# Attention and token mixer on one core: in the first four head pairs the values, with a column of ones, move past standing unnormalised probabilities

## The chip, the core and the metric

The kernel runs on one core of a Trainium2 chip. The metric is the device time of one execution, in microseconds (us). A core has TensorE (PE, its matmuls; PEld, its weight loads), VectorE (DVE), ScalarE (ACT), GpSimd (POOL) and SyncE (SP, which here issues nearly all transfers).

## The reference

Causal attention over 4 batches of 12 heads (448 positions, 64 wide), then a token mixing and a channel mixing over the joined heads:

```python
scores = scale * q @ k.T ; scores above the diagonal = -1e9
attn = exp(scores - max) ; attn = attn / (sum(attn) + 1e-9)
x = heads of (attn @ v) side by side            # [4, 448, 768]
h = relu(x.T @ w_tok1) @ w_tok2 ; u = x + h.T   # 448 -> 256 -> 448
h2 = relu(u @ w_ch1) @ w_ch2 ; out = u + h2     # 768 -> 1536 -> 768
```

All inputs and the output are fp32.

## The kernel before

A list scheduler in the kernel file (class `Plan`) decides the order while the program is built. Every piece of work is a job with a cost per engine that may run it, the jobs it needs, the buffers that it holds and a rank; `emit` walks through modelled time and gives each free engine the ready job of the lowest rank. The table `NUDGE` shifts single ranks, `ONLY` pins single jobs to an engine, and `BIAS`, `FIRST` and `EARLY` say how strongly the plan prefers one engine over another (`FIRST` for jobs whose rank is under `EARLY`). Nothing of the plan runs on the chip: what runs is one fixed order for each engine. Until 75 us of modelled time TensorE gets a filler matmul (line 753, 512 bf16 columns, its result unused) whenever it has no ready job and has done little in the last few microseconds.

The 48 heads are worked on in 24 pairs (`g`), six pairs to a batch. For a pair:

- `load_pair` loads k and q in 32-wide blocks (lines 786) and v (lines 795 and 799, one tile `vraw` of 128 x 4 x 2 x 64); `prep` turns k and q with DVE (line 819).
- `heads`: scores by TensorE (line 849) in 14 pieces, put into four PSUM banks, one to a "round" r; rows 64 wide, so seven pieces c of 64 to 448 columns per pair. DVE scales, masks and takes the minimum of the negated scores (`low`, line 869), ACT takes the exponential in place and adds up the row sums (`expo`, line 881). An exponential with a sum leaves a second instruction on ACT, the accumulator read. Then, twice a pair, `guard` adds 1e-9 to the sums (line 900, or 898 on ACT) and `recip` inverts them (line 903).
- `by_tensor` (pairs 0 to 10): `norm` multiplies each of the seven pieces by its inverse (helper `copy`, line 522 on ACT, 524 on POOL or DVE), `flip` turns four 128 x 128 blocks of a round with TensorE into a bank (line 938), `evac` copies the bank into `pt`. Pairs 11 to 23 go `by_dma` instead.
- `values`: v stands in TensorE as 128 x 64 weights, one head in each half of the columns, and the turned probabilities move past it (line 1039); the output is [2 x 64, 448], channels on the partitions, and `evac` copies it in three pieces into `u`.
- `xturn`: four TensorE transposes of `u` (line 1085), a copy to `xh` and a difference to `xl` (line 533), positions on the partitions. The token matmuls (lines 1133 and 1166, `tokens`) take `xh` and `xl` after every second pair and add to `u`.

When a batch is through its six pairs, `split_u` and `channels` follow (line 1216), whose weights are loaded, converted, and written to a scratch in DRAM on the first use; for the last two batches products of sums of blocks are used (lines 1544 and 1635), and `finish` and `store` write the output.

Of the kernel before, what the change touches and what calls it, by code (L numbers as in the profile page):

```python
# [9 lines left out]
F32 = mybir.dt.float32  # L10
# [11 lines left out]
    "clear": {0: 1.17, 2: -0.46},  # L22
    "load_pair.blocks": {-2: -36.88, 0: 0.42, 6: -1.83, 8: 0.8, 10: 3.87, 12: 1.06, 16: 2.76, 18: 0.85, 20: 8.68,
        22: -5.03, 24: 1.22, 26: -13.46, 28: 25.22, 30: -1.36, 32: 0.08, 34: 2.56, 36: 1.63, 38: 0.03, 40: 4.62,
        42: 2.27, 44: 0.42},
    "load_pair.load": {0.5: 0.54, 2.5: 1.48, 4.5: 1.15, 8.5: 2.41, 10.5: -0.33, 12.5: -7.52, 14.5: -0.58,
        16.5: -0.42, 18.5: 0.8, 22.5: 4.72, 24.5: 5.31, 28.5: -0.38, 30.5: 1.82, 32.5: -1.93, 34.5: 1.62,
        36.5: -0.05, 38.5: -0.47, 40.5: -0.64, 42.5: 13.63, 44.5: -0.01, 46.5: -5.64},
    "narrow.load": {3.5: -0.17, 14: -19.05, 15: 3.09, 16: -4.11, 17: -9.28, 18: -1.53, 19: -0.04, 20: -13.62,
        22: -44.59, 23: 1.48, 24: 0.92, 25: -16.05, 26: -9.5, 28: 1.34, 29: -8.76, 30: -1.29, 31: 0.94, 32: -31.49,  # L30
        33: 0.91, 34: -1.47, 35: 12.16},
    "narrow.size": {3.5: 0.1, 12: 0.33, 13: 13.22, 15: -4.37, 17: 5.83, 18: 4.82, 19: -8.41, 20: 0.23, 21: 3.09,
        24: 9.62, 25: -4.57, 26: 24.43, 27: -9, 28: -32.9, 30: 16.89, 31: -1.07, 33: -5.06, 34: -0.96, 35: -12.41},
# [1714 lines left out]
```

## Time and profile before

| | us |
|---|---|
| median of 3 runs | 557.0 (556.42 to 558.07) |
| the profiled execution, its own time | 558.41 |
| its span, first to last instruction | 556.6 |
| busy PE / DVE / ACT / POOL | 546.4 / 420.6 / 328.0 / 165.3 |

The profile gives one execution. A busy PE counts fillers as well, and its matmuls are pipelined, so their recorded lengths overlap; steps between starts say more. "Idle before" is the time that an engine stood still ahead of an instruction, with what ended it. Lines are those of the kernel before.

### The profile page before, as it was taken

To read this page: it belongs to the slowest core of one execution; us is meant where nothing else is said; L and a number is where in the kernel's file an instruction comes from. 1 tells how busy PE (TensorE), PEld (TensorE's weight loads), DVE (VectorE), ACT (ScalarE), POOL (GpSimd) and SP (SyncE) were. 2 spreads that over 40 slices of the span, in tenths; PEclk is the share of its full clock that TensorE was granted. 3 is DMA by queue.
4 is the path that set the end of the run, shared out by engine and by line. 5 is a ranking of instruction groups with operands and counts; after the bars stand their busy time and mean duration, and the time that the engine had idled before them with its cause. 6 is when DMAs were issued, how large, how long until landed. Compare 5 with 4: busy or idle time off the path is not lost.

```text
span 556.6 us, 10289 instructions
## 1 busy us (share of the span) xinstructions
PE 546.4 (98%) x3470; PEld 461.7 (83%) x3475; DVE 420.6 (76%) x1002; ACT 328.0 (59%) x780; POOL 165.3 (30%) x256
## 2 busy tenths in 40 slices
PE   8998999999999999999999999999999999999997
PEld 4676887788888888877898888989999999999996
DVE  4777768778888877677887868798888859583855
ACT  4998888897785668779878695342232413140400
POOL 3363886355144223324033363133000011020000
PEclk9999999999999999999999999999999999999999
DMA  6777585698999798898999983179411111111137
GB/s 111 166 159 139 107 202 137 144 201 178 222 214 195 171 189 173 189 173 213 190 194 237 202 189 134 44 156 188 105 57 58 57 58 57 58 57 58 57 66 133
DMA packets 234724, 78.41 MB, mean 141 GB/s; under 512 B 208944, under 2 KB 224176, under 8 KB 234672
## 3 DMA queue, kind: packets, MB, share of 16 engines
q1 hardware_dynamic: 223056, 76.15, 62.2%
q10 hardware_dynamic: 11616, 1.61, 1.7%
q8 instruction: 27, 0.44, 0.3%
q14 instruction: 25, 0.20, 0.1%
HBM read 49.15 MB, written 14.94 MB: 115 GB/s over the span
## 4 chain that ended last, share of the span: by engine, by line
PE 80%; DMA 7%; DVE 5%; ACT 3%; SPq 2%; issue 2%; POOL 1%; ACTq 0%; DVEq 0%; POOLq 0%
PE ps L1216 25%; PE ps L1635 14%; PE ps L1544 12%; PE ps L1039 7%; PE ps L849 5%; PE ps L1166 4%; PE ps L1133 4%; DMA wraw<-in_moe_w_ch_dram 4%; PE ps L938 3%; PE ps L1615 3%; PE ps L1085 2%; PE ps L753 2%; SPq L786 2%; DMA out_dram<-kq 1%; DVE prob L869 1%
## 5 line engine op out<-in xcount | busy, mean ns | idle before, releaser
L1283 DVE TENSOR_TENSOR u<-ps,u 128x448 f32<-128x448 f32 x118 | 72.8, 621 | 39.7 <-PE ps L1635 31.0
L881 ACT ACTIVATE prob<-prob,stat 128x448 f32<-128x448 f32 (+6 forms) x168 | 83.7, 503 | 12.7 <-DVE stat L869 12.3
L869 DVE CUSTOM_DVE_ANT_0 prob<-ps,mask 128x448 f32<-128x448 f32 (+6 forms) x168 | 63.0, 415 | 11.5 <-PE ps L849 9.6
L524 POOL TENSOR_SCALAR prob<-prob,stat 128x448 f32<-128x448 f32 (+6 forms) x109 | 60.9, 575 | 32.0 <-DVE stat L903 26.6
L1216 PE MATMUL ps<-uh,wh 128*128 128x448 f32 x144 | 54.4, 378 | 0.2 <-POOL wh L524 0.2
L1216 PE MATMUL ps<-gh,wh 128*128 128x448 f32 x144 | 53.7, 373 | 0.0
L1216 PE MATMUL ps<-uh,wl 128*128 128x448 f32 x144 | 52.7, 366 | 0.3 <-DVE wl L533 0.3
L1216 PE MATMUL ps<-gh,wl 128*128 128x448 f32 x144 | 52.8, 367 | 0.1
L1216 PE MATMUL ps<-gl,wh 128*128 128x448 f32 x144 | 52.8, 366 | 0.0
L1216 PE MATMUL ps<-ul,wh 128*128 128x448 f32 x144 | 52.6, 366 | 0.0
L849 PE MATMUL ps<-kq,kq 64*64 64x448 f32 (+6 forms) x672 | 46.4, 387 | 2.8 <-DVE kq L819 1.5
L1039 PE MATMUL ps<-pt,vraw 128*64 128x448 f32 (+3 forms) x384 | 47.4, 386 | 0.6 <-ACT pt L522 0.4
L522 ACT ACTIVATE wh<-wf 128x768 fp32r<-128x768 f32 x23 | 19.1, 841 | 46.3 <-PE ps L1635 29.1
L1039 PEld LDWEIGHTS ps<-pt,vraw 128*64 128x64 f32 x384 | 25.9, 136 | 23.5 <-issue 12.3
L849 PEld LDWEIGHTS ps<-kq,kq 64*64 64x64 f32 x672 | 27.8, 132 | 20.8 <-issue 10.5
L528 ACT COPY pt<-pt 128x512 uint16<-128x512 uint16 (+1 forms) x50 | 38.8, 851 | 2.4 <-DMA pt<-prob 2.4
L522 ACT ACTIVATE u<-wf 128x768 fp32r<-128x768 f32 (+1 forms) x17 | 12.6, 749 | 37.1 <-PE ps L1544 18.3
L900 POOL TENSOR_SCALAR stat<-stat 128x3 f32<-128x3 f32 (+1 forms) x38 | 10.5, 276 | 77.6 <-ACT prob L881 69.9
L524 POOL TENSOR_SCALAR wh<-wf 128x768 fp32r<-128x768 f32 x19 | 17.1, 900 | 55.3 <-DVE wf L592 24.3
L533 POOL TENSOR_TENSOR wl<-wf,wh 128x768 fp32r<-128x768 f32 x14 | 26.5, 1889 | 22.2 <-ACT wh L522 21.4
L881 ACT ACTIVATION_READ_ACCUMULATOR prob<-prob,stat 128x1 f32 x168 | 32.4, 193 | 0.0
L528 ACT COPY prob<-prob 128x1024 uint16<-128x1024 uint16 x31 | 31.7, 1042 | 0.4 <-POOL prob L524 0.3
(209 smaller groups left out, 1431.7 us busy)
## 6 DMA issues: line engine op xcount, KB each, us to landing
wraw<-in_moe_w_ch_dram SPq DMA_DIRECT2D x24, 768.0 KB, 5.6
wf<-scratch SPq DMA_DIRECT2D x30, 384.0 KB, 3.4
scratch<-wf SPq DMA_DIRECT2D x24, 384.0 KB, 5.7
vraw<-in_v_dram SPq DMA_DIRECT2D x48, 96.0 KB, 2.8
kq<-in_k_dram SPq DMA_DIRECT2D x60, 56.0 KB, 4.4
kq<-in_q_dram SPq DMA_DIRECT2D x56, 56.0 KB, 2.5
gh<-in_k_dram SPq DMA_DIRECT2D x36, 56.0 KB, 2.4
gl<-in_q_dram SPq DMA_DIRECT2D x36, 56.0 KB, 2.5
```

The lines of the kernel that those rows point to most:

```text
L522: nc.scalar.activation(dst, src, AF.Copy, scale=scale)
L524: eng[e].tensor_scalar(dst, src, scale, 0.0, op0=ALU.mult, op1=ALU.add)
L528: nc.scalar.copy(out, in_)
L533: eng[e].tensor_tensor(dst, a, b, op=ALU.subtract)
L849: nc.tensor.matmul(scores[r].tile[lanes, WHERE[c]:WHERE[c] + wide(c)], lhsT=qe.tile[LANES[j], c * QC:(c + 1) * QC], rhs=ke.tile[LANES[j], ...
L869: nc.vector.tensor_tensor_reduce(out=part(c, r), in0=ps.tile[:, WHERE[c]:WHERE[c] + wide(c)], in1=mask[:, S - wide(c):], scale=-SCALE, sca ...
L881: nc.scalar.activation(part(c, r), part(c, r), AF.Exp, bias=stat.tile[:, 0, AT[c]:AT[c] + 1], scale=-1.0, accum_out=stat.tile[:, 1, AT[c]: ...
L1039: nc.tensor.matmul(ps.tile[LANES[j], c * QC:(c + nq) * QC], lhsT=s.tile[:, kb, j], rhs=view[:, o:o + nq, j], start=(kb == 0), stop=(n == 3),)
L1216: nc.tensor.matmul(ps.tile[:, :S], lhsT=x.tile[:, at_:at_ + P], rhs=y, start=(n == 0 and i == 0), stop=(n + 1 == w[2] and i == 2),)
L1283: eng[e].tensor_tensor(u, ps.tile[:, :S], u, op=ALU.add)
L1544: nc.tensor.matmul(ps.tile[:, :S], lhsT=l()[:, t * P:(t + 1) * P], rhs=r, start=(t == 0 and n == 0), stop=(t == half - 1 and n == 2),)
L1635: nc.tensor.matmul(ps.tile[:, :S], lhsT=l.tile[:, t * P:(t + 1) * P], rhs=r.tile, start=(n == 0), stop=(n == 3 * len(fs) - 1),)
```

## The change

For the pairs below `ROWS = 4` the row sums leave the exponentials, and `guard`, `recip` and the seven `norm`s go from between exponential and flip. The flipped, unnormalised blocks are written into `pt` in another layout, in which each 128 x 128 block of keys by queries is contiguous for a head. In the new `by_rows`, in place of `values` and `xturn`, these blocks are the standing operand and v moves past them: 20 matmuls of 65 columns, since v has a 65th column of ones, whose products are the row sums. The output has queries on the partitions, 4 x 65 columns to a bank, two banks to a pair. `guard` and `recip` work on those sums, and `norm` multiplies while it copies out of PSUM (one DVE instruction or four on ACT a bank). The result `x` lies in SBUF as `xturn` used to make it, so `xh` and `xl` are taken from there; four transposes and one copy make `u`. The ring of `stat` has four buffers for two; a kind of PSUM share "r" is added; the plan's preferences and the tables `NUDGE` and `ONLY` are other ones through the whole kernel.

```diff
@@ the tables NUDGE and ONLY: most entries redrawn @@
 NUDGE = {
-    "clear": {0: 1.17, 2: -0.46},
...
+    "by_rows.norm": {0: 12.57, 2: 1.57, 4: -6, 6: 2.02},
...
 ONLY = {
-    "by_tensor.evac": {0: "act", 16: "act", 20: "act"},
+    "by_rows.guard": {0: "act", 2: "act", 4: "act"},
+    "by_rows.hi": {-1: "act", 5: "pool"},
+    "by_rows.lo": {-1: "pool", 1: "pool", 3: "dve", 5: "pool"},
+    "by_rows.evac": {1: "dve"},
+    "by_rows.norm": {4: "dve", 6: "act"},
+    "by_rows.none": {5: "pool"},
...
@@ -241,9 +263,9 @@
-    BIAS = {"act": 200.0, "dve": 600.0, "pool": 0.0}
-    FIRST = {"act": 400.0, "dve": 600.0, "pool": 450.0}
-    EARLY = 3.5
+    BIAS = {"act": 175.0, "dve": 550.0, "pool": 0.0}
+    FIRST = {"act": 250.0, "dve": 350.0, "pool": 600.0}
+    EARLY = 6.0
@@ -474,14 +496,15 @@
+    STATS = 4
-    BUFS.update(stat=2, u=B, xh=1, xl=1, h1h=1, h1l=1, uh=NB, ul=NB, gh=NB * NF, gl=NB * NF)
+    BUFS.update(stat=STATS, u=B, xh=1, xl=1, h1h=1, h1l=1, uh=NB, ul=NB, gh=NB * NF, gl=NB * NF)
-    SHARE = {"s": 4, "t": 2, "a": 1, "m": 3, "w": 5}
+    SHARE = {"s": 4, "t": 2, "a": 1, "r": 2, "m": 3, "w": 5}
@@ -732,6 +755,10 @@
+    ROWS = 4
+    FROM = ((0,), (15, 17), (3, 6, 9), (4, 7, 10, 13))
+    INTO = (slice(5, 17, 3), slice(1, 13, 3), slice(0, 12, 3), slice(15, 19))
+    VW = D + 1
@@ -767,7 +794,8 @@
-        keep["vraw", n] = const.tile([P, NCH, 2, D], F32, tag=f"vraw_{n}", name=f"vraw_{n}")
+        keep["vraw", n] = const.tile([P, NCH, 2, VW], F32, tag=f"vraw_{n}", name=f"vraw_{n}")
+        nc.gpsimd.memset(keep["vraw", n][:, :, :, D:], 1.0)
@@ -793,11 +821,11 @@
-                        out=s.tile[:, :full, j, :],
+                        out=s.tile[:, :full, j, :D],
-                    out=s.tile[:TAIL, full], in_=src[b, 2 * t:2 * t + 2, full * P:].rearrange("h p d -> p h d")
+                    out=s.tile[:TAIL, full, :, :D], in_=src[b, 2 * t:2 * t + 2, full * P:].rearrange("h p d -> p h d")
@@ heads: the exps, and no guard and reciprocal for g < ROWS @@
                 def expo(e, c=c, r=r):
                     nc.scalar.activation(
                         part(c, r), part(c, r), AF.Exp, bias=stat.tile[:, 0, AT[c]:AT[c] + 1], scale=-1.0,
-                        accum_out=stat.tile[:, 1, AT[c]:AT[c] + 1],
+                        **({} if g < ROWS else {"accum_out": stat.tile[:, 1, AT[c]:AT[c] + 1]}),
                     )
                 a = plan.job({"dve": 82.0 + 0.975 * wide(c)}, low, [m, start], [ps, probs[r], stat], rank)
                 if start is None:
                     start = a
-                exps.append(plan.job({"act": 277.0 + 0.857 * wide(c)}, expo, [a], [probs[r], stat], rank))
+                exps.append(plan.job(
+                    {"act": (85.0 if g < ROWS else 277.0) + 0.857 * wide(c)}, expo, [a], [probs[r], stat], rank
+                ))
+            if g < ROWS:
+                rcs[r], exps = exps, []
+                continue
             for rg in RG:
                 if r == rg[-1]:
                     ats = [AT[c] for x in rg for c in ROUND[x]]
@@ -907,6 +940,7 @@
+        stats[g] = stat
@@ -920,8 +954,8 @@
         done = []
         prev = None
         for r, cs in enumerate(ROUND):
-            norms = []
-            for c in cs:
+            norms = list(rcs[r]) if g < ROWS else []
+            for c in cs if g >= ROWS else ():
                 def norm(e, c=c, r=r):
                     copy(e, part(c, r), part(c, r), stat.tile[:, 2, AT[c]:AT[c] + 1])
@@ -943,6 +977,10 @@
+                if g < ROWS:
+                    to = heads_of(pt)[:, :, INTO[r]].rearrange("p j n q -> p n j q")
+                    copy(e, to, ps.tile.rearrange("p (n j q) -> p n j q", n=4, j=2))
+                    return
@@ -953,7 +991,15 @@
+        if g < ROWS:
+            done.append(plan.job(
+                {"pool": 250.0}, lambda e: nc.gpsimd.memset(heads_of(pt)[:, :, 13], 0.0), done[:1], [pt], rank
+            ))
+    def heads_of(pt):
+        return pt.tile.rearrange("p b n q -> p (b n q)").rearrange("p (j o q) -> p j o q", j=2, q=QC)
@@ -1061,6 +1108,116 @@
+    def by_rows(g):
+        b, t = divmod(g, NT)
+        hf, o = divmod(t, NTH)
+        rank = 2.0 * g + RV
+        s, js = raws[g, "v"]
+        pt, pdone = turned.pop(g)
+        stat = stats.pop(g)
+        if t == 0:
+            utile[b] = slot("u")
+        u = utile[b]
+        if o == 0:
+            xs[b, hf] = slot("xh"), slot("xl"), []
+        sh, sl, done = xs[b, hf]
+        n = NCH * P
+        prev = None
+        ready = []
+        def view(s):
+            if o == 0 and s.tile is None:
+                make(s, [P, NCH, PART], F32R)
+            return s.tile[:, :, o * P:(o + 1) * P].rearrange("p (i m) d -> p i m d", i=2)
+        def x():
+            return heads_of(pt)[:, :, 15:19].rearrange("p i (m j) d -> p i m (j d)", m=2)
+        for i in range(2):
+            ps = share("r")
+            def pv(e, i=i, ps=ps):
+                bank(ps)
+                cols = heads_of(pt).rearrange("p j o q -> p j (o q)")
+                for m in (2 * i, 2 * i + 1):
+                    for j in range(2):
+                        to = (2 * (m % 2) + j) * VW
+                        for kb, at in enumerate(FROM[m]):
+                            w = cols[:, j, at * QC:(at + 2) * QC]
+                            nc.tensor.matmul(
+                                ps.tile[:, to:to + VW], lhsT=w, rhs=s.tile[:, kb, j],
+                                start=(kb == 0), stop=(kb == m),
+                            )
+            def guard(e, i=i, ps=ps):
+                sums = ps.tile[:, :4 * VW].rearrange("p (a w) -> p a w", w=VW)[:, :, D]
+                at = stat.tile[:, 1, 4 * i:4 * i + 4]
+                if e == "act":
+                    nc.scalar.activation(at, sums, AF.Copy, bias=1.0e-9)
+                else:
+                    nc.vector.tensor_scalar(at, sums, 1.0e-9, None, op0=ALU.add)
+            def recip(e, i=i):
+                nc.vector.reciprocal(stat.tile[:, 2, 4 * i:4 * i + 4], stat.tile[:, 1, 4 * i:4 * i + 4])
+            def norm(e, i=i, ps=ps):
+                to = x()[:, i].rearrange("p m (j d) -> p (m j) d", j=2)
+                by = ps.tile[:, :4 * VW].rearrange("p (a w) -> p a w", w=VW)[:, :, :D]
+                f = stat.tile[:, 2, 4 * i:4 * i + 4]
+                if e == "dve":
+                    nc.vector.tensor_tensor(to, by, f.unsqueeze(2).broadcast_to([P, 4, D]), op=ALU.mult)
+                else:
+                    for n in range(4):
+                        copy(e, to[:, n], by[:, n], f[:, n:n + 1])
+            prev = plan.job({"pe": (6, 14)[i] * 125.0}, pv, js + pdone + [prev], [ps, s, pt, stat], rank)
+            a = plan.job({"act": 100.0, "dve": 95.0}, guard, [prev], [ps, stat], rank)
+            a = plan.job({"dve": 85.0}, recip, [a], [stat], rank)
+            ready.append(plan.job({"act": 4 * 118.0, "dve": dve1(4 * D)}, norm, [a], [ps, stat, pt], rank))
+        rank = 2.0 * g + RX
+        def hi(e):
+            copy(e, view(sh), x())
+        def lo(e):
+            minus(e, view(sl), x(), view(sh).bitcast(F32))
+        ps = share("t")
+        def turn(e):
+            bank(ps)
+            for m in range(NCH):
+                at = min(m * P, S - P)
+                nc.tensor.transpose(ps.tile[:, at:at + P], x()[:, m // 2, m % 2], ident)
+        def evac(e):
+            if t == 0:
+                make(u, [P, NT, S], F32)
+            copy(e, u.tile[:, t], ps.tile[:, :S])
+        first = [u_ready[b, 0]] if t else []
+        a = plan.job({"pe": pe(0, 0, 0, 0)}, turn, ready, [ps, pt], rank, turn=True)
+        u_ready[b, t] = plan.job({"act": act_ps(S), "dve": dve1(S)}, evac, [a] + first, [ps, u], rank)
+        c = plan.job(
+            {"act": act_sb(n), "dve": dve2(n), "pool": pool1(n)}, hi, ready + done[:1], [pt, sh], rank, lock=True
+        )
+        d = plan.job({"dve": dve1(n), "pool": pool2(n)}, lo, [c] + done[1:2], [pt, sh, sl], rank, lock=True)
+        done += [c, d]
+        if o == NTH - 1:
...
@@ -1702,8 +1859,11 @@
-        values(g)
-        xturn(g)
+        if g < ROWS:
+            by_rows(g)
+        else:
+            values(g)
+            xturn(g)
```

## Rows read from the trace of the kernel before

**Rows 1.** Busy time of each engine by stretch, granted clock, DMA

```profile
6.82:26.84 20.02, 18.71 (x174) 11.68 (x175) 14.81 (x64) 17.41 (x58) 6.02 (x14) 1.00 0.73 150
26.84:57.00 30.16, 27.91 (x266) 20.00 (x264) 23.66 (x94) 27.06 (x90) 15.83 (x35) 1.00 0.71 145
57.00:540.00 483.00, 481.65 (x2960) 417.09 (x2960) 371.17 (x824) 282.21 (x634) 139.73 (x187) 1.00 0.63 141
540.00:556.60 16.60, 12.71 (x65) 11.04 (x63) 9.65 (x19) 0.00 (x0) 0.00 (x0) 0.96 0.74 131
```

**Rows 2.** The same stretches, filler matmuls alone (line 753): PE, PEld

```profile
6.82:26.84 20.02, 5.60 (x22) 2.09 (x23) 1.00 0.73 150
26.84:57.00 30.16, 2.01 (x7) 0.88 (x9) 1.00 0.71 145
```

**Rows 3.** PE in order of time: start, length, line, [idle before <-releaser]

```profile
8.49 1.47 PE L753 MATMUL ps<-mask 128*128 128x512 bf16 x6
11.06 1.09 PE L849 MATMUL ps<-kq,kq 64*64 64x448 f32 x12 [1.09 <-DVE stat L903]
12.08 0.66 PE L938 MATMUL ps<-ident,prob 128*128 128x128 f32 x4
...
16.30 1.09 PE L849 MATMUL ps<-kq,kq 64*64 64x448 f32 x12 [0.16 <-DVE kq L819]
...
22.27 1.24 PE L753 MATMUL ps<-mask 128*128 128x512 bf16 x5
...
24.96 1.95 PE L1039 MATMUL ps<-pt,vraw 128*64 128x448 f32 x16
26.84 1.75 PE L849 MATMUL ps<-kq,kq 64*64 64x448 f32 x28
...
40.37 0.77 PE L1085 MATMUL ps<-ident,u 128*128 128x128 f32 x4 [0.75 <-DVE u L524]
...
51.62 1.09 PE L849 MATMUL ps<-kq,kq 64*64 64x448 f32 x12 [1.30 <-DVE kq L819]
```

**Rows 4.** ACT, DVE and POOL in order of time, first pair

```profile
8.61 0.67 ACT L881 ACTIVATE prob<-prob,stat 128x448 f32<-128x448 f32 x1 [4.54 <-DVE stat L869]
9.19 0.19 ACT L881 ACTIVATION_READ_ACCUMULATOR prob<-prob,stat 128x1 f32 x1
9.28 0.60 ACT L881 ACTIVATE prob<-prob,stat 128x384 f32<-128x384 f32 x1
...
10.45 0.24 POOL L900 TENSOR_SCALAR stat<-stat 128x3 f32<-128x3 f32 x1 [5.89 <-ACT prob L881]
...
11.16 1.00 POOL L524 TENSOR_SCALAR prob<-prob,stat 128x448 f32<-128x448 f32 x2 [0.47 <-DVE stat L903]
```

**Rows 5.** Groups by line, first 75 us: busy us, mean ns

```profile
L881 ACT ACTIVATION_READ_ACCUMULATOR prob<-prob,stat 128x1 f32 x56 | 10.9, 194 | 0.0
L524 POOL TENSOR_SCALAR prob<-prob,stat 128x448 f32<-128x448 f32 (+6 forms) x35 | 17.6, 519 | 8.2 <-DVE stat L903 8.2
L522 ACT ACTIVATE prob<-prob,stat 128x384 f32<-128x384 f32 (+5 forms) x13 | 6.2, 504 | 0.0
L903 DVE RECIPROCAL stat<-stat 128x3 f32<-128x3 f32 (+1 forms) x15 | 2.3, 163 | 0.3 <-POOL stat L900 0.2
L524 DVE TENSOR_SCALAR u<-ps 128x256 f32<-128x256 f32 (+2 forms) x9 | 2.2, 301 | 0.2 <-PE ps L1039 0.2
```

**Rows 6.** Single weight loads and narrow matmuls in order of time

```profile
18.99 0.28 PE L1039 MATMUL ps<-pt,vraw 128*64 128x64 f32 x4
19.04 0.23 PE L1039 MATMUL ps<-pt,vraw 128*64 128x64 f32 x2
19.20 0.20 PEld L938 LDWEIGHTS ps<-ident,prob 128*128 128x128 f32 x2
19.26 0.25 PEld L938 LDWEIGHTS ps<-ident,prob 128*128 128x128 f32 x2
```

**Rows 7.** DVE in order of time: the turn of the fourth pair's q

```profile
25.94 0.65 DVE L819 STREAM_TRANSPOSE kq<-gl 128x448 f32<-128x448 f32 x1 [0.59 <-DMA gl<-in_q_dram]
```

More of the change, by code (lines that the diff above doesn't have):

```diff
@@ L29 @@
[L29 to L33, printed above, removed]
@@ new lines @@
+    "by_rows.none": {1: -3.02, 5: 4.57},
+    "tokens.tok1": {4.5: 0.45, 8.5: -7.6, 12.5: 18.35, 16.5: -3.76, 20.5: -0.04, 24.5: 2.1, 28.5: 6.85, 32.5: 34.5,
+        36.5: 0.83, 40.5: -6.33, 44.5: -0.03, 48.5: -10.19},
+    "tokens.relu": {-5: 1.89},
+    "tokens.lo": {-5: -1.47},
+    "tokens.plus": {-5: -0.02},
+    "by_rows.twice": {5: 2.24},
+    "tokens.tok2": {8.5: -7.84, 12.5: -3.52, 16.5: -4.03, 20.5: 2.43, 24.5: 8.09, 28.5: -0.92, 32.5: 1.73,
+        40.5: 0.87, 44.5: 4.29, 48.5: 0.74},
@@ new lines @@
+    "channels.relu": {-6: 11.02},
+    "channels.down": {28.5: -29.26, 28.75: 0.16, 29: 0.23, 29.25: 2.64, 29.5: -4.01, 29.75: 4.65, 36: 0.22,
[5 rows of a table added]
+    "add.plus": {-6: 24.05},
+    "store.turn": {-5: 35.2},
+    "store.send": {-5: -4.69},
+    "reread.load": {-4.95: 1.16, -4.94: 0.34, -4.92: 6.14, -4.91: -0.19, -4.9: 3.76},
+    "group.up": {54: 17.53, 54.18: 5.85, 54.54: -1.47, 54.9: -7.06, 74.25: 12.25, 74.43: -3.66, 74.61: -9.5,
+        74.79: 0.12, 74.97: 0.12, 75.15: -0.81},
+    "hidden.relu": {-6: -0.57},
@@ L147 @@
+    "spared.hi": {-4.9: -12.62},
+    "spared.lo": {-4.9: -0.23},
+    "finish.plus": {-6: 1.64},
+    "finish.turn": {-6: -3.91},
+    "finish.evac": {-6: -1.13},
+    "finish.send": {-6: 2.16},
 }
@@ new lines @@
+    "heads.guard": {10: "pool", 14: "dve", 16: "pool", 20: "dve", 22: "dve", 24: "act", 30: "act", 32: "pool",
+        34: "pool", 42: "pool", 44: "pool", 46: "act"},
+    "xturn.<lambda>": {9: "dve", 19: "dve", 21: "dve", 27: "act", 31: "act", 33: "act", 39: "act", 43: "dve",
+        45: "act"},
+    "split_u.hi": {12.5: "act", 36.5: "act"},
+    "split_u.lo": {12.5: "pool", 36.5: "dve", 48.5: "dve"},
+    "by_tensor.norm": {14: "pool", 18: "pool", 20: "act"},
+    "xturn.twice": {13: "act", 17: "pool", 33: "act"},
@@ L1018 @@
     turned = {}
+    stats = {}
     def values(g):
@@ L1063, in values, with twice, none @@
         u_ready[b, t] = plan.job({"act": 110.0 + act_ps(S), "dve": 120.0 + dve1(S)}, evac, [prev] + first, [ps, u], rank)
+    def by_rows(g):
[80 more added lines that the diff above has]
+        if o == NTH - 1:
+            def twice(e):
+                x = sh.tile[:, NCH - 1]
+                copy(e, x[:TAIL], x[P - TAIL:].bitcast(F32))
+            def none(e):
+                x = sl.tile[:TAIL, NCH - 1]
+                copy(e, x, mask[:TAIL, :PART])
+            c = plan.job({"act": act_sb(PART), "pool": pool1(PART)}, twice, done[:], [sh], rank)
+            done += [c]
+            done += [plan.job({"act": act_sb(PART), "pool": pool1(PART)}, none, done[:], [sl], rank)]
```

213 lines of the change are left out of this document (100 added, 113 removed), and 47 rows, old and new, of the table NUDGE.

## The prediction, made before the change was run

> **What bounds the kernel now.** I read the busy times by stretch first [rows 1]. From 57 to 540 us TensorE stands still for 483.00 - 481.65 = 1.35 us at a granted clock of 1.00 (2.4 GHz), so there only less TensorE work would help, and the change takes none away. The tail, 540 to 556.6, stands still for 3.9 us behind the last additions and stores; the change does not touch it. What can be won lies before 57 us. There I took the fillers out [rows 2]: 22 in the first stretch, 7 in the second. Five in a row last 1.24 us [rows 3], of which the last one's own length overlaps; the step is about 0.215, so they cover 4.7 and 1.5 us. With the idle time (20.02 - 18.71 = 1.3 and 30.16 - 27.91 = 2.25) TensorE does nothing useful for 6.0 us between 6.8 and 26.84 and for 3.75 us between 26.84 and 57: 9.8 us in all. That is the most that an earlier supply of the first pairs can give.
>
> Then the order in time says what is late [rows 3]. After the first scores there are fillers from 8.49 and a stand until 11.06; the first flip comes at 12.08. The other engines tell why [rows 4]: the first exponential runs from 8.61 to 9.28, but its flip waits for three exponentials with their reads, for the guard at 10.45, an inverse, and the norm on POOL at 11.16. ACT is busy for 17.41 of the 20.02 us of that stretch [rows 1], so there the softmax sets the pace, not TensorE. In the second stretch two stands end otherwise: at 40.37 on a copy of values by DVE, at 51.62 on k and q just turned by DVE [rows 3], that is, on loads.
>
> **The change, part by part.**
>
> *TensorE, values.* Before, a pair takes from 24.96 to 26.84, 1.88 us [rows 3], as 16 records: an fp32 matmul leaves two, and the two heads share the array. After, there are 20 matmuls with 128 x 128 fp32 weights, thus 40 loads and 40 records of 65 columns, one behind the other. No row has 128 weight columns with so few moving ones, so I bound the step. From below by the moving columns: 64 of them step from 18.99 to 19.04 [rows 6], so 65 take about 0.055, 2.2 us a pair. From above by a transpose, which pairs the same 128 x 128 fp32 load with 128 columns: the loads at 19.26 and the next one, whose two take 0.25 us together where one takes 0.20 - 0.06 = 0.14, stand 0.11 us apart [rows 6], 4.4 us a pair. Between them: the first two loads of that flip start at 19.20 and 19.26 [rows 6], 0.06 apart, with nothing moving yet that the second would wait for. That is the nearest to a load alone, so I take 0.06: 2.4 us a pair, 0.52 more than before, **+2.1 us** for four pairs (bounds +1.3 and +10.1).
>
> The Trainium skill, "TensorE: Matmul & The Clock Gate", section "LDWEIGHTS (loading the stationary operand)", lets a load take its columns divided by 1.2 in nanoseconds, 107 for 128 columns; by it the term would be (40 x 0.107 - 1.88) x 4 = +9.6 us and the whole sum +3.4, 560.4, close to the upper bound. The trace has a second such load started 0.06 us after the first [rows 6], which speaks against it, though a load that starts early could still be slow to end.
>
> *TensorE, the rest.* Flips stay four a round and the four transposes stay; +0. Instead of turning probabilities for the values, nothing else is added.
>
> *ACT.* 28 accumulator reads go (7 x 4 pairs). A read lasts 0.194 [rows 5], but it starts 0.09 before its exponential ends and the next starts 0.10 before the read ends [rows 4], so each step shrinks by about 0.10: 2.7 us in all (at most 5.4).
>
> *Norms.* 28 of the seven-piece norms go. In the first 75 us POOL ran 35 for 17.6 us and ACT 13 for 6.2 us [rows 5]; at 0.5 each, 28 are 14 us of engine time, by their shares about 10 on POOL and 4 on ACT. In return DVE or ACT multiplies 256 PSUM columns twice a pair. The nearest row is DVE's copy of values, 0.30 for pieces of 64 to 256 columns [rows 5]; I take 0.4, so 8 x 0.4 = 3.2 us on DVE, which is busy for 14.81 of 20.02 [rows 1] and hides it; without that room, as much is late on `x`, and behind it the token matmuls. Bounds: 0.3 and 1.0 (four ACT pieces). Guard and inverse (0.16 [rows 5]) stay two each a pair, only later in the chain; the three copies of values into `u` become one.
>
> *No cost that I count:* a memset per pair on POOL and two for the ones at the start, since POOL is idle for 14 us of the first stretch [rows 1]; the 65-wide `vraw`, whose transfers keep their pieces of 256 bytes; `xh` and `xl` out of SBUF in place of PSUM. The stat ring of four can only take a wait away. No transfer is added.
>
> *What the path gains.* The first flip can follow its exponential, at about 9.5 instead of 12.08. For each of the four pairs the guard, the inverse and the norm (0.24 + 0.16 + 0.5, with waits of 0.5 us for the inverse [rows 4]) come out from between exponential and flip, and go behind the values. ACT, the pacing engine, loses 2.7 + 4 = 6.7 us of work in the opening. I reckon that the first stretch recovers 4.9 of its 6.0 us: all but some 1.1 us around the first exponential, where TensorE has nothing but q and k that are not there yet. TensorE's work for pairs 0 to 2, 3 x (1.75 scores + 4 x 0.45 flips + 2.4 values + 0.5 transposes) = 19.4 us, fits into the 20 us until pair 3's q is turned at 25.94 to 26.6 [rows 7]. In the second stretch the stands on loads remain; I take 1.3 of 3.75.
>
> **Sum.** 2.1 - 4.9 - 1.3 = -4.1 us. The profiled execution took 558.41 us (span 556.6 and 1.8 around it), 1.4 above the median of the runs shown; -4.1 makes 554.3 of it and 552.9 of the median 557.0. I predict 553.0. The redrawn order of all later work can move the 1.35 and 3.9 us of stands after 57 us by perhaps 1.5 either way.
>
> **The rivals.**
>
> *A. The weight loads bind: slower.* With a load every 0.11 us, as in the flips [rows 6], the values cost 4.4 us a pair. With the same recovery the sum is 10.1 - 6.2 = +3.9: 560.9. It decides from 0.086 us a load on, where 4 x (40 x 0.086 - 1.88) eats the 6.2 us. For it: in every transpose load and matmul step together at 0.11. Against it: the 0.06 of the first two loads, and that 128 moving fp32 columns explain the 0.11 alone, twice the 0.05 of 64 columns [rows 6]. It is the case that the Trainium skill's rule ("TensorE: Matmul & The Clock Gate") describes.
>
> *B. The loads pace the opening: the gain is given back.* What is done earlier before 26.84 becomes a longer wait for pairs 4 to 6, whose k and q come when they came before. If all 4.9 us of the first stretch return as waits before 57, the sum is 2.1 - 1.3 = +0.8: 557.8. For it: the stands at 16.30 and 51.62 end on DVE's turn of new q or k [rows 3], and pair 3's q ended 0.59 us of DVE's idling [rows 7]. Against it: behind the opening lie the token matmuls, which wait for no load of q or k, and from 57 us on TensorE has more work than it can do [rows 1], so work pulled forward has a backlog to start on.
>
> *C. The waits were not the softmax's.* If the copies out of PSUM and the token weights on ACT hold the flips, half is recovered: 2.1 - 3.1 = -1.0, 556.0. For it: ACT still has exponentials and copies in the same queue. Against it: 12.08 against 9.28 for the first flip, where no such copy stands before it.
>
> **How the numbers follow.** Chances: the forecast 0.62, A 0.12, B 0.14, C 0.12. The forecast's own range is 550.5 to 555.2 (recovery of 4.5 to 8, the order +-1.5). The range over the cases is 549.0 to 559.0: below, 8 us recovered at the lower price of the values with the order in its favour (557.0 - 8 + 1.3 - 1.5 = 548.8); above, B with the order against it; it leaves out most of A. Two measurements of this kernel can be told apart from about 0.3%, 1.7 us. The forecast is faster; B and C within 0.3%, but for a 0.02 of B that the order makes slower; A is slower: 0.62, 0.24, 0.14.
>
> **What the profile would show.** Right: far fewer than 29 fillers and 3.5 us of idling between 6.8 and 57 us; the first flip before 10 us; 40 value loads of a pair in about 2.4 us; the first channel matmul some 4 us earlier. Wrong: value records that step at 0.11 (A); the stands before 57 grown and ended by turns of k or q (B); the same fillers with flips released by ACT copies (C). A granted clock below 1.00 in the opening, where fewer fillers run, would break all of it: at half the clock each microsecond of such a stretch costs half of one.

## The result: slower, 561.05 us against 557.18

The changed kernel took 561.05 us (median of 7, 559.7 to 561.95), the kernel before 557.18 beside it: 1.0061 of before, 95% interval 1.0035 to 1.0087. By the medians that is 3.9 us slower (3.4 by the ratio, 1.9 to 4.8 by its interval), where 553.0 was predicted. The profiled execution took 559.93 us, 1.1 under its median; its span is 558.1.

Windows of the changed kernel, columns as in [rows 1], and under "..." those of its fillers alone (line 780; columns as in [rows 2]). In its line numbers 877 are scores, 909 exponentials, 972 flips, 1149 values, 1194 the four transposes and 847 DVE's turns of k and q; in other runs the lines shift by a few.

```profile
6.82:26.84 20.02, 19.02 (x199) 15.86 (x199) 14.09 (x56) 15.44 (x41) 4.69 (x7) 1.00 0.74 163
26.84:57.00 30.16, 30.16 (x286) 25.94 (x287) 21.22 (x83) 24.70 (x77) 15.36 (x29) 1.00 0.63 125
57.00:540.00 483.00, 483.00 (x3003) 416.96 (x2996) 384.94 (x869) 291.95 (x659) 110.36 (x138) 1.00 0.64 141
...
6.82:26.84 20.02, 1.19 (x4) 0.39 (x4) 1.00 0.74 163
26.84:57.00 30.16, 3.41 (x12) 1.17 (x12) 1.00 0.63 125
```

Idle time and fillers (0.215 us each) before 57 us fell from 9.75 us to 1.0 + 0 + 16 x 0.215 = 4.4. Taken alone this looks like the forecast come true: 5.3 us recovered, 6.2 predicted. (One of the 29 fillers counted before had started at 6.51, ahead of the first scores, so it is 0.2 less.) But TensorE is full of something else. Its order in time:

```profile
6.96 1.75 PE L877 MATMUL ps<-kq,kq 64*64 64x448 f32 x28 [0.69 <-DVE kq L847]
9.56 0.63 PE L972 MATMUL ps<-ident,prob 128*128 128x128 f32 x4 [0.86 <-ACT prob L909]
...
23.09 4.58 PE L1149 MATMUL ps<-vraw,pt 128*128 128x65 f32 x40
27.51 0.60 PE L972 MATMUL ps<-ident,prob 128*128 128x128 f32 x4
...
73.81 0.47 PE L1373 MATMUL ps<-uh,wh 128*128 128x448 f32 x1
```

The first flip comes at 9.56 in place of 12.08 [rows 3]; about 9.5 was forecast. The granted clock of both stretches is 1.00, as before. The values of a pair take from 23.09 to 27.51, 4.42 us, not 2.4: with 1.88 before [rows 3], +10.2 us for four pairs. The first channel matmul starts at 73.81; before it was 74.75 (the 74.75 line below). So 0.9 us of the 4 forecast are there. The weight loads of this kernel by line and form (busy us, mean ns | idle before), values first:

```profile
L1149 PEld LDWEIGHTS ps<-vraw,pt 128*128 128x128 f32 x160 | 18.3, 192 | 0.4 <-ACT pt L545 0.3
L972 PEld LDWEIGHTS ps<-across_ident,prob 128*128 128x128 f32 x88 | 10.1, 142 | 1.3 <-issue 0.6 <-ACT prob L909 0.2
```

A value load of 128 columns is recorded as 0.19 us long and the next starts about 0.11 us later (4.42 / 40); the flips' loads, from which the prediction took its price, are recorded as 0.14.

From the trace of before, two lines that the prediction did not use, the start of its channel matmuls (order in time) and ordinary fp32 loads of 128 columns (groups by form):

```profile
74.75 0.47 PE L1216 MATMUL ps<-uh,wh 128*128 128x448 f32 x1
```

```profile
L1133 PEld LDWEIGHTS ps<-xl,w1hi 128*128 128x128 f32 x96 | 18.3, 191 | 0.1
```

Apart from those of transposes, every 128 x 128 fp32 load of before is recorded as 187 to 191 ns long. So the trace of before already told these loads from the flips'; but neither recorded length is the step of 0.11.

### The profile page after: what moved, and what is told of

It is laid out like the page before. It is cut to its first block, busy times and chain, and to the rows that moved or that the text cites. A ratio compares the mean times of both kernels' runs of the same rounds, so it can differ in the third digit from the quotient of the medians.

```text
span 558.1 us, 10391 instructions
## 1 busy us (share of the span) xinstructions
PE 549.7 (98%) x3554; PEld 471.4 (84%) x3554; DVE 430.4 (77%) x1027; ACT 333.4 (60%) x775; POOL 134.5 (24%) x198
## 4 chain that ended last, share of the span: by engine, by line
PE 96%; DMA 1%; ACTq 1%; DVE 0%; issue 0%; ACT 0%; DVEq 0%
PE ps L1373 32%; PE ps L1792 15%; PE ps L1701 11%; PE ps L877 8%; PE ps L1086 7%; PE ps L1290 6%; PE ps L1323 5%; PE ps L972 4%; PE ps L1149 3%; PE ps L1772 3%; PE ps L1242 2%; ACTq L1846 1%; DMA kq<-in_q_dram 1%; PE ps L780 1%; DMA out_dram<-kq 1%; PE ps L1194 0%
## 5 line engine op out<-in xcount | busy, mean ns | idle before, releaser
L1373 PE MATMUL ps<-gh,wh 128*128 128x448 f32 x144 | 53.6, 372 | 0.0
L877 PE MATMUL ps<-kq,kq 64*64 64x256 f32 (+6 forms) x672 | 46.7, 388 | 0.7 <-DVE kq L847 0.7
L551 ACT COPY pt<-pt 128x512 uint16<-128x512 uint16 (+1 forms) x57 | 45.3, 865 | 3.4 <-DMA pt<-prob 3.4
L545 ACT ACTIVATE wh<-wf 128x768 fp32r<-128x768 f32 x20 | 16.5, 839 | 43.2 <-PE ps L1792 32.6
L1086 PE MATMUL ps<-pt,vraw 128*64 128x448 f32 (+3 forms) x320 | 39.5, 387 | 0.0
L547 POOL TENSOR_SCALAR prob<-prob,stat 128x448 f32<-128x448 f32 (+6 forms) x60 | 34.7, 593 | 18.1 <-DVE stat L936 18.0
L1086 PEld LDWEIGHTS ps<-pt,vraw 128*64 128x64 f32 x320 | 21.1, 136 | 19.5 <-issue 11.9
L556 POOL TENSOR_TENSOR wl<-wf,wh 128x768 fp32r<-128x768 f32 x15 | 28.6, 1907 | 35.4 <-ACT wh L545 34.5
L1792 PE MATMUL ps<-u,wh 128*128 128x448 f32 x108 | 30.9, 367 | 0.0
L1373 PEld LDWEIGHTS ps<-uh,wh 128*128 128x128 f32 x144 | 27.0, 188 | 3.4 <-issue 1.1
L1373 PEld LDWEIGHTS ps<-gh,wh 128*128 128x128 f32 x144 | 27.1, 188 | 2.8 <-DVE u L1331 0.2
```

The costliest lines, as they stand in the source:

```text
L547: eng[e].tensor_scalar(dst, src, scale, 0.0, op0=ALU.mult, op1=ALU.add)
L551: nc.scalar.copy(out, in_)
L556: eng[e].tensor_tensor(dst, a, b, op=ALU.subtract)
L877: nc.tensor.matmul(scores[r].tile[lanes, WHERE[c]:WHERE[c] + wide(c)], lhsT=qe.tile[LANES[j], c * QC:(c + 1) * QC], rhs=ke.tile[LANES[j], ...
L1086: nc.tensor.matmul(ps.tile[LANES[j], c * QC:(c + nq) * QC], lhsT=s.tile[:, kb, j, :D], rhs=view[:, o:o + nq, j], start=(kb == 0), stop=(n ...
L1373: nc.tensor.matmul(ps.tile[:, :S], lhsT=x.tile[:, at_:at_ + P], rhs=y, start=(n == 0 and i == 0), stop=(n + 1 == w[2] and i == 2),)
```

## The experiments

Ratios are to the kernel before, run on the same chip, with their 95% intervals. Some kernels keep the order of all instructions and change only what an instruction is; those are compared most directly. Where the planner had to draw another order, it is said.

**1. What a value load costs.** The changed kernel with its first four pairs' value matmuls in four forms, and then halves in all four pairs:

```diff
 (changed kernel, by_rows, pv)
-  matmul(ps.tile[:, to:to + VW], lhsT=w, rhs=s.tile[:, kb, j], ...)
+  for h in LANES:      # weights in two halves of 64 columns
+      matmul(ps.tile[h, to:to + VW], lhsT=w[:, h], rhs=s.tile[:, kb, j], ...)
```

> The changed kernel, its value matmuls of the first four pairs in four widths: pair 0 moves 33 columns (half the channels are left out), pair 1 moves 65 as before, pair 2 moves 128 (both heads, so its values are other numbers), pair 3 moves 65 columns past each 128 x 128 block given as two blocks of 64 weight columns in the two halves of the array. Theory (the loads of 128 fp32 weight columns set the step): 0.11 us a record in pairs 0, 1 and 2 alike, so 40 records in 4.4 to 4.5 us each, and 0.056 us for the two halves together in pair 3, as in the kernel before, 2.2 to 2.3 us for 80 records. Rival (the moving columns, or a fixed cost of each matmul, set the step): by columns 0.057 : 0.112 : 0.22 us in pairs 0, 1, 2 and no gain in pair 3; by a fixed cost per record 0.11 in pairs 0, 1, 2 and 0.22 for the two halves in pair 3.

One execution took 558.83. Its value matmuls in order of time: pair 0 moves 33 columns, pair 1 65, pair 2 128; pair 3 has halves.

```profile
16.85 3.21 PE L1150 MATMUL ps<-vraw,pt 128*128 128x33 f32 x28
23.07 4.58 PE L1166 MATMUL ps<-vraw,pt 128*128 128x65 f32 x40
39.42 3.39 PE L1155 MATMUL ps<-vraw,pt 128*128 128x128 f32 x28
48.99 2.55 PE L1161 MATMUL ps<-vraw,pt 128*64 128x65 f32 x80
```

28 records last 3.21 us with 33 columns and 3.39 with 128: the columns that move are nearly free. Twice as many records with half the weight columns take 2.55 us where 40 whole ones take 4.58, so it is no fixed cost of each record either. The load theory holds.

> The changed kernel in the same order, but in all four pairs each 128 x 128 block stands as two blocks of 64 weight columns, one in each half of the array. Theory (the weight loads of the values are what made the change slower): 2.2 us less TensorE work a pair, 9 us in all; all of it lies before 57 us, where the order has fillers left, and shows at the end nearly in full: 552 to 554 us, ratio to the kernel before 0.990 to 0.995. Rival (the redrawn order of the rest, or the tail, made it slower): the values are faster, but the end stays at 558 to 561, ratio 1.00 to 1.006.

558.62 (median of 12), 1.0040 (1.0024 to 1.0055). The theory (552 to 554) failed; the time lies where the rival had it. The values now cost 2.5 to 2.6 us a pair, close to the 2.4 that the prediction assumed and to the 20 x 0.125 us by which the plan drew this order, and the time is still 2.2 us over before, not 4 under. Some 7.5 us of TensorE time went, and the end came only 1.7 us earlier by the medians (1.2 by the ratios, whose intervals overlap). So the load price alone does not explain the miss: a second step failed. TensorE by stretch, and what it waited for:

```profile
6.82:26.84 20.02, 17.93 (x294) 1.00 0.75 155
26.84:57.00 30.16, 26.84 (x358) 1.00 0.69 134
```

```profile
27.02 0.66 PE L972 MATMUL ps<-across_ident,prob 128*128 128x128 f32 x4 [1.35 <-ACT prob L909]
...
44.47 1.09 PE L877 MATMUL ps<-kq,kq 64*64 64x448 f32 x12 [0.30 <-DVE kq L847]
...
54.97 1.09 PE L877 MATMUL ps<-kq,kq 64*64 64x448 f32 x12 [1.73 <-DVE kq L847]
```

2.1 and 3.3 us of idling, with the same 16 fillers (3.4 us): 8.2 to 8.9 of the 9.75 us of before are back (three of the 16 filler matmuls are not in the trace and may be counted as idling too). In the changed kernel they were missing because dear values filled them. In the two stretches ACT's exponentials end 2.2 us of stands, turns of k and q 2.0.

**2. Does TensorE work in the opening reach the end at all?** Before, with 12 more fillers a pair, 10.3 us, put in at the values of the first four pairs:

> The kernel before with 12 more filler matmuls (2.6 us at 0.215) ahead of the values of each of the first four pairs, 10.3 us in all: the TensorE time that the weight loads of the changed kernel add, in the old order. Theory (the opening has waits that take up most of added TensorE work): +3 to +6 us, ratio 1.005 to 1.011. Rival (TensorE is the bound there too, each us lands at the end): +9 to +10.3 us, ratio 1.016 to 1.019.

565.44, 1.0159 (1.0135 to 1.0182): 8.9 of the 10.3 us arrive, nearly the rival's 9 to 10.3, and the theory failed. TensorE time that is added at the values of the old order reaches the end; in the changed kernel's order, where 7.5 us taken away gave back 1.2 to 1.7, most of it came back as stands.

**3. What holds the opening: the softmax or the loads?** One part taken away at a time, the order kept:

```diff
 in heads and by_tensor, no normalisation for g < 4 (its jobs stay, but issue nothing)
-  accum_out=stat.tile[:, 1, AT[c]:AT[c] + 1],
+  **({} if g < 4 else {"accum_out": stat.tile[:, 1, AT[c]:AT[c] + 1]}),
...
+  if g < 4: return      # in guard, recip and norm
 in load_pair, light loads for pairs 1 to 6
+  if 0 < g < 7:
+      eng[e].dma_start(out=s.tile.rearrange("p c d -> p (c d)"),
+          in_=src[b, 2 * t:2 * t + 2].rearrange("j (a x) d -> (j a) (x d)", x=7))
+      return
   for n in range(4):    # four strided transfers
```

> The kernel before in its own order, with the row sums, the additions to them, the inverses and the seven multiplications of the first four pairs left out, so these pairs stay unnormalised. It shows what the softmax's waits are worth without any TensorE cost. Theory (the opening waits for these steps): the idle 1.3 us of the first stretch and part of the 2.25 us of the second go, but the fillers, which are fixed in the order, stay: -1 to -3 us, ratio 0.995 to 0.998. Rival (the opening is paced by loads and by copies out of PSUM): no change, ratio 0.999 to 1.001.

> The kernel before, its order the same, with k and q of pairs 1 to 6 read by one transfer in DRAM order (rows of 1792 bytes) in place of four in blocks of 128 bytes; these pairs work on other numbers. SyncE's issue time falls from 2.0 to about 0.5 us a load, and the transfer itself is shorter. Theory (the loads pace the opening; what TensorE gains or loses there is taken from or given to waits on them): the stands that end on DVE's turns of k and q go, 2 to 4 us, ratio 0.993 to 0.997. Rival (the order of ACT, DVE and POOL paces it): under 1 us, ratio 0.999 to 1.001.

> The changed kernel with the same light loads for pairs 1 to 6. There TensorE has only 4.4 us of fillers and idling left between 6.8 and 57 us. Theory (loads pace the opening, but here the slow values fill most of the wait): 0 to 2 us less than the changed kernel, ratio 1.002 to 1.006. Rival (loads do not matter): ratio 1.006.

> The changed kernel with the values' blocks standing as two halves of 64 columns and with the light loads. Theory (the 7.5 us that the halves take from TensorE came back as waits on loads): the waits shrink and the end follows, 3 to 6 us less than with the halves alone, ratio 0.993 to 0.998. Rival (the fixed order of the other engines holds TensorE): no change against the halves alone, ratio 1.003 to 1.005.

> The kernel before with two things left out at once: k and q of pairs 1 to 6 come by one contiguous transfer each (they hold other rows than the reference's), and the sums, guards, inverses and norms of the first four pairs are dropped (their rows stay unnormalised). The first alone gave 552.8 (0.9929 of before), the second alone 1.0005. Theory (two bounds, one behind the other: the softmax's chain is worth nothing as long as the loads pace the opening, and shows once they do not): 551.5 or less, 0.9905 of before or below. Rival (the softmax's chain is hidden even then, since the order on the engines is fixed and fillers stand in it): 552.3 to 553.3, the same as with light loads alone.

| | us | ratio |
|---|---|---|
| before without the normalisation | 557.05 | 1.0005 (0.9988 to 1.0022) |
| before with light loads | 552.80 | 0.9929 (0.9905 to 0.9953) |
| changed with light loads | 561.35 | 1.0080 (1.0054 to 1.0106) |
| halves with light loads | 554.04 | 0.9952 (0.9934 to 0.9969) |
| before, light loads, no normalisation | 554.05 | 0.9955 (0.9938 to 0.9972) |

Taking away the whole normalisation, more than the change does, gives nothing in the order of before, with ordinary loads or light ones. Light loads give 3.7 us to before and 4.6 to the halves (4.9 by the ratios), and nothing to the changed kernel, whose TensorE is full. The last one came out above both of its expectations, so the theory of two bounds in a row fell: behind the loads the normalisation is not the next.

Fillers could have hidden this, since they stand in the fixed order whether something is late or not. So the same without the 28 behind the first scores:

> The kernel before, in its own order, without the 28 filler matmuls behind the first 15 (those ahead of the first scores stay). Nothing is left out of the result. If the clock holds, every wait that a filler covered now shows with what ends it. Theory (the fillers only fill time that k, q and their transposes need anyway): 555.5 to 557.5, no change, most of the stands before 57 us ended by DVE's turns of k and q. Rival (the fillers themselves are in the way: they cost some 6 us where the softmax is already done): 552 to 554, and stands that are left end on flips' exponentials or norms. If the granted clock falls, over 558, and the other two comparisons are against this run.

> The run before this one (no fillers after the first scores), and the sums, guards, inverses and norms of the first four pairs dropped, so that their rows stay unnormalised. If the softmax's chain is late in the opening of before (as the prediction said), then with no filler in its place 4 to 5 us go: 551 to 553, if the run before is at 556.5. If k and q are late, no more than 1.5 us go.

> The kernel before without fillers after the first scores, and k and q of pairs 1 to 6 by one contiguous transfer each (other rows than the reference's). If k and q are late: 4 to 7 us less than without fillers alone, 550 to 552.5. If the softmax is late: no more than 1.5 us less.

> The changed kernel with value weights in halves, without the fillers behind the first 15. Nothing is left out of the result. Theory (loads pace its opening): 557 to 559, as with fillers (558.6), and the stands before 57 us end on DVE's turns of k and q. Rival (its fillers are in the way of work that is ready): 554 to 556.

| without fillers | us | ratio |
|---|---|---|
| before | 554.85 | 0.9975 (0.9956 to 0.9994) |
| before, no normalisation | 556.65 | 1.0006 (0.9984 to 1.0027) |
| before, light loads | 551.95 | 0.9924 (0.9901 to 0.9948) |
| halves | 559.16 | 1.0047 (1.0024 to 1.0071) |

Again the loads count and the normalisation does not. Before without fillers lies between its two expectations; light loads bring 2.9 us there, less than the 4 to 7 expected and more than the rival's 1.5; the halves end just above theirs. Without the normalisation the time is even 1.8 us longer than without fillers alone; the mean granted clock of these executions is lower too (0.995 against 0.997), and no run shows what else there is to it. TensorE by stretch in before without fillers, then also without the normalisation, then with light loads (length, PE and other engines busy, granted clock):

```profile
6.82:26.84 20.02, 14.86 (x146) 9.92 (x140) 14.86 (x64) 17.48 (x57) 6.06 (x14) 0.91 0.75 153
26.84:57.00 30.16, 27.57 (x272) 20.51 (x269) 23.83 (x94) 27.57 (x93) 16.09 (x36) 1.00 0.72 147
```

```profile
6.82:26.84 20.02, 14.94 (x159) 9.79 (x161) 13.88 (x57) 14.42 (x36) 2.71 (x6) 1.00 0.74 153
26.84:57.00 30.16, 26.74 (x262) 19.96 (x255) 23.08 (x89) 23.92 (x73) 11.33 (x25) 1.00 0.72 146
```

```profile
6.82:26.84 20.02, 14.51 (x158) 9.62 (x160) 15.64 (x67) 17.85 (x61) 7.02 (x16) 1.00 0.55 160
26.84:57.00 30.16, 29.95 (x287) 23.12 (x286) 25.08 (x98) 29.46 (x98) 18.18 (x42) 1.00 0.61 143
```

In the first stretch, where the prediction hoped for 4.9 us, TensorE stands for 5.2, 5.1 and 5.5 us: neither the normalisation nor the light loads empty it. In the second the light loads bring 2.6 us down to 0.2. Of what stays in the first stretch, 2.50 us are explained below, and 1.6 to 2.1 us end on an ACT copy of flipped blocks into `pt`.

Why the normalisation does not count is best seen at the stand ahead of pair 1's scores. TensorE in before without fillers, then the same without the normalisation:

```profile
10.84 1.09 PE L854 MATMUL ps<-kq,kq 64*64 64x448 f32 x12 [2.50 <-DVE stat L908]
...
51.22 1.09 PE L854 MATMUL ps<-kq,kq 64*64 64x448 f32 x12 [2.12 <-DVE kq L824]
```

```profile
11.59 1.09 PE L854 MATMUL ps<-kq,kq 64*64 64x448 f32 x12 [2.50 <-DVE kq L824]
...
51.14 1.09 PE L854 MATMUL ps<-kq,kq 64*64 64x448 f32 x12 [1.72 <-DVE kq L824]
```

The stand is 2.50 us either way. With the inverse gone, its releaser is called by another name: the turn of pair 1's q. That is what scores need; they never needed an inverse. With the fillers in place it is the same: the 1.09 us of [rows 3] stay when the normalisation goes:

```profile
11.63 1.09 PE L849 MATMUL ps<-kq,kq 64*64 64x448 f32 x12 [1.09 <-DVE kq L819]
```

DVE's queue in the kernel before shows why (order in time):

```profile
10.09 0.35 DVE L869 CUSTOM_DVE_ANT_0 prob<-ps,mask 128x192 f32<-128x192 f32 x1
10.37 0.08 DVE L869 DVE_READ_ACCUMULATOR2_ANT stat<- 128x1 f32 x1
10.37 0.64 DVE L819 STREAM_TRANSPOSE kq<-gl 128x448 f32<-128x448 f32 x1
10.93 0.13 DVE L903 RECIPROCAL stat<-stat 128x3 f32<-128x3 f32 x1
```

Seven minima, which the change keeps, run from 7.95 to 10.45, then the turn of q, and the small inverse behind it ended last. This one stand is DVE's order; it stays 2.50 us with light loads too. The later ones (51.22, 51.14) are k and q that come late; without fillers and with light loads TensorE idles for only 30.16 - 29.95 = 0.2 us between 26.84 and 57.

In the changed order ACT has a share as well: in the halves without fillers its exponentials end 3.5 us of stands before 57, turns of k and q 3.0. The halves with light loads idle for 1.7 us there, not 5.4, and what is left ends on exponentials.

The traces also show SyncE's queue, which the loads share with v and the token weights. The loads of a later pair in before, then with light loads (start, length of the issue):

```profile
34.11 2.15 SPq L786 DMA_DIRECT2D gh<-in_k_dram  x4
36.30 2.38 SPq L786 DMA_DIRECT2D gl<-in_q_dram  x4
```

```profile
31.86 0.58 SPq L785 DMA_DIRECT2D gh<-in_k_dram  x1
32.50 0.42 SPq L785 DMA_DIRECT2D gl<-in_q_dram  x1
```

Up to 57 us the issues of SyncE add up to 53.6 us in before and 53.2 in the halves, nearly without a pause; with light loads they are 34.7 and 36.5. Light loads free the queue for the others behind them too: the first token weight is issued at 6.87, not 13.29. So they show what the loads are worth together, not k and q alone.

**4. The redrawn order.** The edit with halves, in the planner's preferences and tables of before; and q of pairs 1 to 3 issued by ACT (`FIRSTQ = 4` for 1), in the halves and in before. All three make the planner draw a new order with tables that were made for another list of jobs.

> The changed kernel with its value weights in two halves of 64 columns, and with the planner's preferences and both tables of single shifts and pins taken from the kernel before, so that only the edit itself differs from before, not the redrawn order. Theory (the edit adds about 2.5 us of TensorE work, and what it takes out of the softmax's chain does not come back because loads pace the opening; the redrawn order is worth little either way): 557.5 to 560, thus 1 to 3 us over before and like the halves alone (1.0040 of before). Rival (the redrawn order is what lost the time, by its burst of stores at the end, some 1.5 us): under 557, the last stores again issued one by one, and the stretch from the last matmul to the end under 4.2 us.

> The changed kernel with halves, and with q of pairs 1 to 3 issued on ACT's queue instead of SP's, as q of pair 0 is in both kernels: 12 issues of about 0.5 us each leave SP's queue for the first microseconds of ACT, before its first exponential. Nothing is left out. Theory (it is SP's issuing, one transfer every half microsecond, that paces the opening): 555.5 to 557.5, 1 to 3 us less than halves alone (558.6). Rival (the moving of the many short packets paces it, whoever issues): 558 to 559; if ACT's first exponential comes later for it, over 559.

> The kernel before with q of pairs 1 to 3 issued on ACT's queue instead of SP's, nothing left out. Theory (SP's issuing paces the opening of before as well): 554 to 555.8, 0.9955 to 0.9985 of before. Rival (the packets pace it): 556.3 to 557.3, no change; if ACT's first exponential comes later for it, over 557.3.

577.15 (1.0378, 1.0346 to 1.0410), 573.54 (1.0303, 1.0277 to 1.0328) and 578.32 (1.0389, 1.0364 to 1.0415). The first missed both its expectations by far; the others are over the "559" and "557.3" named for a late first exponential, by 15 and 21 us. TensorE's waits in the first of them (us in total, times, longest):

```profile
PE ps L1680 <- ACT u L523: 8.7, 2, 6.0
PE ps L855 <- DVE stat L1142: 2.8, 1, 2.8
```

The largest lies at 405 us, in block products that the edit does not touch. So the redrawn tables are part of the edit: without them it costs 21 us, not 2. That does not price the redrawn order by itself, since these tables were made for another list of jobs; whether a better order would bring the halves under before was not tried. The other two do not tell whether SP's issuing is the pace, since ACT stood in its queue. From before with q on ACT:

```profile
5.65 6.40 ACTq L786 DMA_DIRECT2D gl<-in_q_dram  x8
...
12.07 1.28 ACT L881 ACT_TABLE_LOAD   x1 [12.07 <-DMA gl<-in_q_dram]
```

Eight issues took 6.40 us, not the 4 expected, and the first exponential, at 8.61 before [rows 4], came at 13.37. SyncE's full queue in experiment 3 speaks for issuing as the pace of the loads, but light loads change the packets as well, and no run separates the two.

**5. The tail.** From its last matmul to the end the changed kernel needs 4.9 us in its trace, before 3.3: the last copy waits for an earlier store. The last copy of before, then of the changed kernel:

```profile
553.33 0.42 DVE L524 TENSOR_SCALAR kq<-ps 112x256 f32<-112x256 f32 x1 [0.20 <-PE ps L1663]
```

```profile
554.84 0.42 DVE L547 TENSOR_SCALAR kq<-ps 112x256 f32<-112x256 f32 x1 [1.80 <-DMA out_dram<-kq]
```

The last two copies got buffers of their own; the order stays the same.

```diff
-  pt, o = share("t"), slot("kq")
+  pt, o = share("t"), slot(("xh", "xl")[part] if b == B - 1 else "kq")
```

> The changed kernel, the same instructions in the same order, but the last two copies out of PSUM write into the two buffers of xh and xl, long free by then, instead of two of the five kq buffers. Nothing is left out. Theory (the last copy waits for an earlier store of its kq buffer, so some 1.5 us of the loss sit in the tail): 559 to 560.2, 0.8 to 2 us under the changed kernel (561.05). Rival (the stores share the same queues and DMA engines, and what is waited for at the copy is then waited for at the last store's landing): 560.7 to 561.5, no change.

> The changed kernel with value weights in halves, and the last two copies in buffers of their own as in the run before. Nothing is left out. Theory: 557 to 558, 0.6 to 1.6 us under halves alone (558.62, 1.0040 of before), which leaves less than 1.5 us over before. Rival: 558.3 to 559.

> The kernel before without fillers after the first scores, and the last two copies in buffers of their own. Nothing is left out. Its last copy stood only 0.2 us, for TensorE: both theories expect what the run without fillers gave, 0.9975 of before (554.5 to 555.3), and it is to show that the buffers alone give nothing in that order. It is also the candidate for a kernel faster than both.

560.63 (1.0071, 1.0044 to 1.0097), 557.87 (1.0027, 1.0007 to 1.0047) and, as expected, 555.68 (0.9974, 0.9954 to 0.9994). In the changed kernel the wait goes and the time stays (order in time; then the last stores, with their size and us from issue to landing):

```profile
553.27 0.42 DVE L547 TENSOR_SCALAR xl<-ps 112x256 f32<-112x256 f32 x1 [0.19 <-PE ps L1820]
```

```profile
out_dram<-xh ACTq DMA_DIRECT2D x1, 112.0 KB, 3.6
out_dram<-xl SPq DMA_DIRECT2D x1, 112.0 KB, 3.3
```

The copy is 1.57 us earlier, the span 0.2 shorter (557.9), since the last stores land 3.3 to 3.6 us after their issue; in before the stores of this size take 2.0. The buffer was not the cause; the rival holds. With halves the interval covers both. That the stores land late because the new order issues them in a burst was not tried.

The fastest kernel that leaves nothing out is before without its later fillers, 0.9975 (0.9956 to 0.9994), and 0.9974 with the other buffers.

## Why the prediction was wrong, step by step

Forecast were -4.1 us, measured +3.9: 8.0 us apart. With values at about the forecast price (the halves) it is still +2.2, so some 6.3 of the 8.0 belong to the gain that was not there, and 1.7 (1.2 by the ratios, not clear of their intervals) to the dear loads.

**Values, +2.1 us: the price was wrong.** The step "the nearest to a load alone, so I take 0.06" rested on the starts of the first two loads of a flip [rows 6]. Such a start says when a load began, not how often one can end. The runs show 0.11 us a load whatever moves behind it: 4.42 us a pair, +10.2 us. The upper bound, 4.4, was right, and the rule of the Trainium skill ("TensorE: Matmul & The Clock Gate", "LDWEIGHTS (loading the stationary operand)"), 107 ns for 128 columns, agrees with the 0.11 measured; the argument against it was wrong. The argument that 128 moving columns explain the 0.11 alone fell with the 33 columns of experiment 1. Rival A had this price right, and its 560.9 lies beside the 561.05 measured. But it took the recovery for real as well, so that the two numbers meet is partly luck.

**What the path gains, -6.2 us: failed, and it cost the most.** In the changed kernel 5.3 us of standing are gone, but because dear values filled them: with values at 2.5 us a pair stands and fillers are back at 8.2 to 8.9 us. Such values cost 2.5 to 2.9 us more than before, and +2.2 (1.3 to 3.1) is measured: of the gain nothing is left. The reason given, a softmax that sets the pace, is refuted for the order of before: without normalisation nothing is gained. What the prediction read as the softmax, "a stand until 11.06", was a scores matmul whose releaser had the name of an inverse [rows 3]; scores wait for k and q. ACT's 17.41 of 20.02 us [rows 1] did not show that its normalisation was late; in the redrawn order ACT's exponentials, which the change keeps, do end part of the stands.

**Rival B**, with +0.8, is nearest to the +2.2 of the halves, though under their interval. It was given up because "behind the opening lie the token matmuls, which wait for no load". They wait for values, values for scores, and scores for k and q; with light loads the halves are 4.6 us faster. **Rival C** (copies out of PSUM) was not tested by a run of its own; without fillers one stand of 1.65 us before 57 is ended by such a copy.

**The small terms.** ACT's busy time in the first stretch fell from 17.41 to 15.44 us, with fewer accumulator reads and norms in it. DVE's multiply out of PSUM took 0.41 us (0.4 taken), but for four of the eight banks only; the other four went to ACT in 16 pieces, 0.9 us of busy time a bank, within the bound of 1.0. No run prices these terms at the end.

**The order after 57 us** (1.5 either way): the stands from 57 to 540 went from 1.35 us to 0, the tail grew by 1.6. The two traces cannot divide the 3.9 us: the traced execution of before is 1.2 us over the median beside it, that of the changed kernel 1.1 under, so their spans differ by 1.5 only, and TensorE's last matmul ends at 553.3 and 553.2. Added up from the starts in both, values are +10.2, fillers and stands from the beginning to 57 us -5.5, stands after it -1.35, all other TensorE steps -3.4 and the tail +1.6. Why the other steps are shorter in the redrawn order, no run shows.

## What to carry to other kernels

Price a standing operand by the step of a long row of records that load it, at the same columns and type, and not by the first two starts of a group: with 128 fp32 columns each record costs 0.11 us here, so few moving columns are dear and two halves of 64 cost little more than half. Before a wait is put down to its releaser, ask what the waiting instruction reads, and which instruction of that queue made it; then take the supposed cause away with the order kept. Filled time is not recovered time: see whether the stands come back when the filling is made cheap, and treat a hand-tuned order as part of any edit that changes its list of jobs.

## What was not expected of the hardware

Halves of 64 weight columns, each writing its own half of the partitions, run at 2.55 us for 80 records, 0.03 a record, as if two shared the array; whole ones need 0.11 (experiment 1). In before without fillers, granted clock by stretch (length, PE busy, clock, DMA share, GB/s):

```profile
6.82:10.84 4.02, 1.52 (x28) 1.00 0.61 115
10.84:14.00 3.16, 3.16 (x24) 0.69 0.69 111
```

TensorE was busy for 1.52 of 4.02 us, then the clock fell from its upper level (2.4 GHz) towards the lower (1.2): four transposes took 1.01 us there, 0.60 to 0.66 later. Without the normalisation the same first scores came 0.74 us later (7.34, not 6.60) and were followed by a stand of the same 2.50 us, and the clock stayed at 1.00. So this stand was followed by a fall in one trace and by none in the other; what decided it is not shown.
